# The last jobs of a DCN kernel reordered, its last phase taken into the run, and one group's output turned tile by tile

## The chip, the core and the metric

One Trainium2 chip, one core. The metric is the device time of one execution in microseconds (us), the median of several. An engine here is one of five: PE is TensorE (matmuls), ACT is ScalarE, DVE is VectorE, POOL is GpSimd, SP is SyncE, which in this kernel issues nearly all transfers (DMAs).

## The reference

A deep and cross network: six layers, each multiplies the running x by a weight matrix, adds a bias, multiplies by the first input and adds x.

```python
B, F, D, L = 16384, 26, 16, 6        # x0: 16384 x 416, all bfloat16
x = x0
for l in range(6):
    proj = jnp.einsum('bd,de->be', x, ws[l]) + bs[l]
    x = x0 * proj + x
return x
```

## The kernel before

**Layout.** The 16384 rows are cut into 8 groups of 2048, and x is kept transposed: features on partitions, rows along the free axis. 416 features are three tiles of 128 and a tail of 32. A *job* (g, l) is layer l of group g. It has 3 *tiles* of output features, each of 4 *chunks* of 512 columns (512 rows of the batch). The four 32-feature tails of a group's four chunks share one 128-partition tile `x3s`, one quadrant each. In some layers the quadrants stand rotated, and a copy of the tail is then rotated by two DMAs (`rotate`, lines 444 and 445), issued in `prefill`.

**Evacuation.** A chunk's sum of 13 row matmuls (or 3 full ones and a small one) lands in a PSUM bank. ScalarE adds the bias and writes it to `tw` (lines 514 and 550); VectorE multiplies it by x0 (L523, L562) and adds x (L528, L567). That is the chunk of x for the next layer. Tails go the same way through `ts` (L604 to L612).

**The run.** Most tiles are computed in one long *run* (`stream`). There a chunk isn't four matmuls over the whole array but 13 matmuls of 32 rows by 128 columns (L1040, and L1044 for the tail features), and four such matmuls for different chunks are in work at once, one on each 32-row strip. Which chunk each strip takes next is written out by hand in the string `ORDER`: one letter is one strip's share of one chunk (its letter tells the strip and how many chunks back the chunk was begun), and `|` is a *phase*, at which the tails of a batch of jobs (three, at the end two) are computed in one go (`tails`, L697 and L685). `replay` walks through the string and works out in units of 1/20 of a matmul's time when each letter starts, when each PSUM bank comes free, and so the order in which matmuls are emitted. Its constants (READ, NEXT, SUMS and so on) are the planner's estimates of what an evacuation takes.

The run ends with (7,4) tile 0, the item called `behind`; the last four chunks of the run get their three full-width matmuls behind it (`full`, L650). After the run come five more tiles in whole-array matmuls: (6,5) tiles 0 and 1, a phase with the tails of (7,4) and (6,5), (6,5) tile 2, and (7,4) tiles 1 and 2.

**The last job.** (7,5) is computed the other way round (L1130), with the rows of the batch on partitions, so that its result needs no turning. It multiplies and adds in that layout (`nat_mul`, L1188; `nat_add`, L1194) and stores (`nat_store`, L1201). For its residual it needs x(7,5) turned: tiles 0 and 1 by DMA transposes (`rest_turn`, L928), tile 2 by TensorE (`turn_last`, L1141).

**The outputs.** When the last layer of a group g < 7 is done, `output(g)` turns its three tiles by DMA transposes into `ost` (L880) and the tails into `ot3` (L888); `spread` copies `ot3` into its columns of `ost` on POOL (L909), for group 6 on ACT (L907); `store` writes `ost` to memory (L916). There is one `ost` for all groups. `done_with(g, l)` is called once for a job's tails and once for its tiles, and the second call starts `output`.

**What sets the order.** `Program` keeps one queue for each engine, in the order of the `add` calls, and turns reads and writes of named tokens into semaphore waits. Each engine works its queue in order, so an instruction that waits holds up everything behind it on that engine. For SyncE that means: a DMA whose data isn't ready holds up all later DMAs. In the last part its order is: turns of tiles 0 and 1 of group 6, `ot3`, two half turns of tile 2, two half turns of x(7,5) tile 1, then the two halves of store 6. On ScalarE the spread of group 6 stands between the evacuations of (7,4) tiles 1 and 2.

Of the kernel before, what the change touches and what calls it, by code (L numbers as in the profile page):

```python
# [21 lines left out]
class Program:  # L22
# [176 lines left out]

SLOT = 20  # L200
FENCE, PHASE, CHANGE = 22, 52, 9
READ, NEXT, BACK, SECOND, PAIR, TAILS, SUMS = 19, 56, 70, 92, 56, 220, 240
LETTERS = "ABCDEFGHIJKLMNOPQRSTUVWXYZabcdefghijklmnopqrstuvwxyz0123456789"
ORDER = (
    "ABCDAJCXaFTMWDUNSLYBKTMZjGANDaMpCPUJCXIROEDBaTUJCITVCQLVCAXNaALVaQHNKUTBQKDRICbRK|AJDWQJDCfUNSDM"
    "dSbJECbURCTINWDUJSPAJCTAZSPUJCDVYOTJAaDYVKTENCbNUSDJAXSYJGPAVODNUDOJUTCIRCDUNSbAJTaMVKHQBCXQNCPI"
    "ZSDJQCDMVaTEJOXBUDOAZXOIRGDYBSXARLOYBXKMZG|QBPSIVDCPAZOXQJGDQBaTINCLAdSXJYOHRACTNUCPJUSDAVCXRMaL"
    "FUCXARWPYBKPAdaLUNCLMVTCNISDcBWPIRCLAVSbMBKPYVSHMB|CTMVCPIVCDUNaTIBaTVAKTNUGDMVSDINCXYJCDMVSbIFW"
    "PQBCTMVCPIVSDIBWTANKTYVODAZOTUJGDURODINCbUJODBMSbIVCTUBSPIVGDQVCTMJWDAZSXINGDUBSXIBKTAZKPcRGAZPW"
    "QBP|QBOLRECTBCUPZSAPRaXASJPUBKUDVSAPRKAbSNcDOUbFKDURKDIRCbQJOXBIODVAOTUJCLQVCDUNSbEJWDQVCTINCbUJ"  # L210
    "ODIBaTVAKTNUGDMVSDINCXBcXSNAKPAZWLAVKTYNGDYNSDYN|ICXJTACVQPCNAPeVAPeRYLWNQDKNbCIBWTYBSLMVCLMVCXM"
    "JSDAdWPQBLOQBbKNQCDdMWTZEODNUKTABOXAVCTcVOLERCDcRaPAJWbMRKHYBCXQNCPIZSDJQCDMVaDMJSbAJTOYVGDMVCjU"
    "N|ISDJTAKRMDJCQDNeITVGMbBWIDRWIDRKAbJSMDBObQJCDdOQXJaMDJWMTBKAXhSMDJOUDVKQPFCMDBaQfVKALRWMDJOUDV"
    "KATBOYjREWDROULBKUTBSIBLCUdCMLZSAbJSUDRKMXeFLQBCXMR|CPISFDQCTIBaDUZKDQJWbMBXOIZCLQBSbIdODIVCTUJO"
    "DIVODIBbCNYXKERDCUdTaIBTaJUOHAVCTMVKDUJSDAVCXQNKDYJWfAJWTMZGDMVCXcNS|IDJTECRCTANaDYVKTMFWDUBOXAN"
    "KXZQODZATOJUCLURODINCbIBWTJYOHAVCTMVKDUJSDIRDCUNSbBISbVAKPURCLMRWDINCXIBWTJgOHAVCTMVKDUJSDAVCXQN"
    "KDYJSfAJaPURGDMdCbUN|ISDJTECRCTANaDMVKTFYWDAVOTYJGXAVODNUDOJUTCIRODIBSbUJPCIVDQCZTMBaLMBaXIBWLQZ"
    "ODIZCXQZKPAJWDRMWDNUKTBISBDUORbAOZDaULNQGXJCQXBAWPRaIDRKUDJSUPGBAbVCMDVOYLFSUPBeMXRCM|RCPISFDQCT"
    "IBaTIVOHQBPCMVDOAZWPBUOLQBCfURODIdWPQZGDQNCbINWDINXGQBPAWBQPKVDIVSPAJODYJCXQKZPEBWDQNWLAVKTAJSAD"
    "OVYDNKTYBKbMVSHBeMXRCM|RCPISFDQCDMVaTIBSbUBTKMVCLMVSDIBSXIZDKURDSMJCbIBSXIZOHQBCTMVCPIVSDQJCTIBa"  # L220
    "DUZSLAJbQOVHAOBbUOBLUChTIVOALVOQDJCXQBiLMSVDKMBbWJMHCVASXdIDJSUPCJUDSVIDSBMbRCMLRCcbJOALVMaDJMaD"
    "JYOXRAO|ANXKQBLSABOXYRGLMVDWNACbNQWDNISDJAWfBcSXJMGbVQCPRCPISFDAeTUBKTMVCLUNSDMJTCIBWTIdOHQBPCMV"
    "DOAZWPBUKDQVCfIRWPYFCXQZCPIRWDJQWPEBCTAZSPUJCLAZCXMRaLUBWLAVLSgNXGIRCDUNS|IDJTAKRMDJCQbJWATVCQPJ"
    "WALBaUTBODUadTIGVATVOIDJWAXRKYPFCMDBaMTCZMLRWALRCAfROUDJeUTaBQPKVEDVSMDJOAfJCQXKZMDJWATJWMDVKMTB"
    "CARaXMBKPZUDWRIPaAJbCYVTO|EJDWQBPCNAbOVLQCJDUiRLaAJbSUNDKMXCBMTWJYHOAVPCMVDOUBPWIRDIORXENKLAUKBN"
    "CD"
)


def replay(tails, events, needs, keep, part):  # L230

# [10 lines left out]
    n = len(tails)  # L242
    size = [[(3 if c < n - keep else part) + (r == tails[c]) for r in range(4)] for c in range(n)]
    free, flight, begun, act = [0] * 4, {}, 0, 156
    banks = [(0, 0), (0, 1), (0, 2), (0, 3), (84, 4), (84, 5), (178, 6), (178, 7)]
    home, read, out, latest, due = {}, {}, [], [[]] * 4, list(events)

    def over(now):
        nonlocal act
# [8 lines left out]
    for letter in ORDER:  # L258
        if letter == "|":
            now, m = min(free), due.pop(0)  # L260
            parts = [(f - now) // SLOT for f in free]
            at = now + max((f - now) % SLOT for f in free)
            over(at)
            on = at + 3 * SLOT * m + PHASE
            moved = [on + SLOT * k for k in parts]
            for f in flight.values():
                f[1] = moved[f[2]] if f[1] == free[f[2]] else -9 * SLOT
            got = [banks.pop(0) for _ in range(m)]
            assert all(t <= at + 3 * SLOT * k for k, (t, _) in enumerate(got))
# [12 lines left out]
            out.append([at, -1, [b for _, b in got], on])  # L282
            continue
        age, r = divmod(LETTERS.index(letter), 4)
        c, now = begun - age, free[r]
        over(now)
        if not age:
            t, home[c] = banks.pop(0)
            start, begun = max(now, t), begun + 1
            for t, d in needs[c]:  # L290
                start = max([start] + [read[d + k] + SUMS - SLOT * t for k in range(4)])
            flight[c] = [sum(1 << q for q in range(4) if size[c][q]), 0, r]
        else:
# [12 lines left out]
def bass_standalone__cross_network_dcn__recsys_kernel(  # L306
# [18 lines left out]
             (0, 4), (1, 3), (2, 2), (3, 1), (0, 5), (1, 4), (2, 3), (3, 2), (4, 0), (1, 5),  # L325
             (2, 4), (3, 3), (4, 1), (5, 0)]
    order += [(NG - 1 - g, L - 1 - l) for g, l in reversed(order)]
    order[-6:] = [(5, 5), (7, 3), (6, 4), (7, 4), (6, 5), (7, 5)]
    assert len(set(order)) == NG * L
    cuts = [1, 2, 3] + [3] * 12 + [3, 2]  # L330
    batches = []
# [206 lines left out]
    def evacuate_chunk(g, l, i, j, b, read):  # L538
# [138 lines left out]
    def tails(batch, corners_last=False, banks=None):  # L677
# [26 lines left out]
        if corners_last:  # L704
            corners()
            for k in sorted(range(len(batch)), key=lambda k: k != 1):
                evacuate_tail(*batch[k], bs_[k], vector=k == 1)
                while behind_tail:
                    behind_tail.pop(0)()
        pr.flush()  # L710
        for g, l in batch:
            if corners_last:
                prefill(g, l + 1)
                filled.add((g, l + 1))
            done_with(g, l)
        while later:
            load_group(later.pop(0))
# [155 lines left out]
            add("sp", lambda h, j=j: h.dma_start(brow[j * T32:j * T32 + 1, :], bs[L - 1:L, :]),  # L873
                reads=["brow"], writes=[("brow", j)], lane="brow", batch=0)

    def output(g):

        s, s3 = xset[(g, L)], xtail[(g, L)]
        def turn(t, j0=0, j1=NJ):
            add("sp", lambda h: h.dma_start_transpose(  # L880
                ost[:, j0 * KK:j1 * KK, t * P:(t + 1) * P], xs[s][:, t * GC + j0 * CH:t * GC + j1 * CH]),
                reads=[("x", s, t, j) for j in range(j0, j1)], writes=[("ost", t, j) for j in range(j0, j1)],
                lane="ot" if g < LAST - 1 else f"ot_{t}{j0}", batch=g)
# [4 lines left out]
        add("sp", lambda h: h.dma_start_transpose(ot3[:, :, :], x3s[s3][:, :]),  # L888
            reads=[("x3", s3)], writes=["ot3"], lane="ot3", batch=g)
# [53 lines left out]
        if (jb, i) in where:  # L943
            items.append(("tails", where[(jb, i)]))

    for i in range(1, NT):
        late = items.index(("tile", (LAST, L - 2), i))
        items.append(items.pop(late))


    single = 0
    k = 0
    while k < len(items):
        if items[k][0] == "tails":
            if single % 2 == 0:
                nxt = k + 1
# [48 lines left out]
    def stream(run, keep, part):  # L1005
# [72 lines left out]
    for n, it in enumerate(items):  # L1078
# [200 lines left out]
```

## Time and profile before

| | |
|---|---|
| median of 3 runs | 467.53 us (467.3 to 467.93) |
| profiled execution | 467.5 us, of which 465.7 are the span from first to last instruction |
| run (L1040, L1044), first to last start | 40.74 to 429.14 us |
| start of (7,5) on TensorE | 448.50 us |
| TensorE, VectorE, ScalarE busy | 458.9, 404.2, 379.1 us |
| transfers | 53.77 MB; 256-byte packets from the turns, 832-byte packets from the stores |

Times are counted from the span's start. A line of the timeline reads: start, length, engine, source line, operation, what it writes and reads, count of merged instructions, and in brackets the idle time before it and what ended it. For SPq lines the length is that of the issue on SyncE, not of the transfer; when a transfer lands is read from the semaphore that it raises. PE's ends are modelled, so starts are used for its pace.

### The profile page before, as it was taken

To read this page: it belongs to the slowest core of one execution; us is meant where nothing else is said; L and a number is where in the kernel's file an instruction comes from. 1 tells how busy PE (TensorE), PEld (TensorE's weight loads), DVE (VectorE), ACT (ScalarE), POOL (GpSimd) and SP (SyncE) were. 2 spreads that over 40 slices of the span, in tenths; PEclk is the share of its full clock that TensorE was granted. 3 is DMA by queue.
4 is the path that set the end of the run, shared out by engine and by line. 5 is a ranking of instruction groups with operands and counts; after the bars stand their busy time and mean duration, and the time that the engine had idled before them with its cause. 6 is when DMAs were issued, how large, how long until landed. Compare 5 with 4: busy or idle time off the path is not lost.

```text
span 465.7 us, 17469 instructions
## 1 busy us (share of the span) xinstructions
PE 458.9 (99%) x7827; PEld 263.8 (57%) x7833; DVE 404.2 (87%) x700; ACT 379.1 (81%) x608; POOL 6.8 (1%) x15
## 2 busy tenths in 40 slices
PE   9999999999999999999999999999999999999995
PEld 5444566555556677555655556565575566755442
DVE  2887998989989899979989898888989889898897
ACT  4687888788888888888878888788887887889785
POOL 1000000000000000000000000000000000000000
PEclk9999999999999999999999999999999999999998
DMA  8986949101002978084858437990100095027899
GB/s 229 185 177 144 160 113 190 29 3 26 1 4 38 158 210 155 22 141 149 149 92 154 145 78 141 160 296 23 25 2 4 25 148 172 14 49 169 183 161 292
DMA packets 139087, 53.77 MB, mean 115 GB/s; under 512 B 112762, under 2 KB 138500, under 8 KB 139012
## 3 DMA queue, kind: packets, MB, share of 16 engines
q1 hardware_dynamic: 138856, 52.54, 52.5%
q8 instruction: 61, 1.00, 0.9%
q10 hardware_dynamic: 156, 0.11, 0.1%
q14 instruction: 14, 0.11, 0.1%
HBM read 5.97 MB, written 13.63 MB: 42 GB/s over the span
## 4 chain that ended last, share of the span: by engine, by line
PE 93%; DVE 4%; DMA 1%; issue 1%; ACT 0%; SPq 0%; DVEq 0%
PE ps L1040 70%; PE ps L697 7%; PE ps L1044 6%; PE ps L650 6%; PE ps L638 2%; PE ps L685 1%; DMA wm<-in_ws_dram 1%; DVE x L1194 1%; DVE x L1188 1%; DVE x L528 1%; DVE tw L523 1%; PE ps L671 1%; ACT tw L514 0%; PE ps L789 0%; SPq L734 0%
## 5 line engine op out<-in xcount | busy, mean ns | idle before, releaser
L1040 PE MATMUL ps<-x,wm 32*128 32x512 bf16 x6000 | 356.0, 374 | 0.0
L550 ACT ACTIVATE tw<-ps,bias 128x512 bf16<-128x512 f32 x500 | 310.5, 688 | 46.4 <-PE ps L1040 35.9
L1040 PEld LDWEIGHTS ps<-x,wm 32*128 32x128 bf16 x6000 | 212.5, 92 | 127.7 <-ACT tw L550 4.1
L562 DVE TENSOR_TENSOR tw<-tw,x 128x1024 bf16<-128x1024 bf16 x250 | 168.2, 689 | 39.6 <-ACT tw L550 38.9
L567 DVE TENSOR_TENSOR x<-tw,x 128x1024 bf16<-128x1024 bf16 x250 | 163.5, 690 | 0.3
L1044 PE MATMUL ps<-x,w 32*128 32x512 bf16 x504 | 151.7, 374 | 0.0
L1044 PEld LDWEIGHTS ps<-x,w 32*128 32x128 bf16 x504 | 42.7, 92 | 6.6
L514 ACT ACTIVATE tw<-ps,bias 128x512 bf16<-128x512 f32 (+1 forms) x46 | 35.0, 839 | 12.0 <-PE ps L671 7.9
L650 PE MATMUL ps<-x,wm 128*128 128x512 bf16 x146 | 33.6, 379 | 1.0 <-issue 0.8
L697 PE MATMUL ps<-x,wm 128*32 128x512 bf16 x564 | 33.6, 380 | 0.0
L608 ACT ACTIVATE ts<-ps,bias 128x512 bf16<-128x512 f32 x33 | 21.0, 687 | 14.7 <-PE ps L685 14.7
L523 DVE TENSOR_TENSOR tw<-tw,x 128x1024 bf16<-128x1024 bf16 (+1 forms) x35 | 21.4, 627 | 4.9 <-ACT tw L514 4.7
L650 PEld LDWEIGHTS ps<-x,wm 128*128 128x128 bf16 x152 | 13.9, 98 | 19.0 <-issue 3.2
L697 PEld LDWEIGHTS ps<-x,wm 128*32 128x32 bf16 x564 | 13.5, 96 | 18.7 <-ACT tw L550 4.7
L528 DVE TENSOR_TENSOR x<-tw,x 128x1024 bf16<-128x1024 bf16 (+1 forms) x35 | 20.6, 624 | 0.0
L612 DVE TENSOR_TENSOR x<-ts,x 128x512 bf16<-128x512 bf16 x47 | 18.4, 420 | 0.4
L610 DVE TENSOR_TENSOR ts<-ts,x 128x512 bf16<-128x512 bf16 x33 | 13.0, 418 | 0.0
L604 DVE SCALAR_TENSOR_TENSOR ts<-ps,bias,x 128x512 bf16<-128x512 f32 x14 | 10.5, 748 | 2.2 <-PE ps L685 2.2
L909 POOL COPY ost<-ot 128x512 bf16<-128x512 bf16 x6 | 5.3, 890 | 411.3 <-DMA ot<-x 411.3
L1130 PE MATMUL ps<-wm,x 128*128 128x416 bf16 x48 | 9.8, 340 | 0.1
L1182 ACT ACTIVATE x<-ps 128x416 bf16<-128x416 f32 x16 | 7.6, 518 | 2.4 <-PE ps L1130 2.4
L799 DVE COPY x<-ps 128x512 bf16<-128x512 bf16 x5 | 2.0, 423 | 8.5 <-PE ps L789 8.5
(50 smaller groups left out, 76.9 us busy)
## 6 DMA issues: line engine op xcount, KB each, us to landing
out_dram<-ost SPq DMA_DIRECT2D x6, 1664.0 KB, 7.1
x<-x SPq DMA_DIRECT2D x24, 96.0 KB, 2.3
x<-in_x_dram SPq DMA_DIRECT2D x8, 208.0 KB, 4.4
x<-in_x_dram SPq DMA_DIRECT2D x4, 416.0 KB, 8.0
out_dram<-ost SPq DMA_DIRECT2D x2, 832.0 KB, 6.0
wm<-in_ws_dram SPq DMA_DIRECT2D x5, 312.0 KB, 3.4
x<-x SPq DMA_DIRECT2D x22, 64.0 KB, 2.0
out_dram<-x SPq DMA_DIRECT2D x3, 416.0 KB, 4.8
```

The source lines that it names most:

```text
L514: add("act", lambda h, a=a, w=w, b0=b0: h.activation(tw[r][:, a * CH:(a + w) * CH], psum[:, b0 * CH:(b0 + w) * CH], ACT_F.Identity, bias=b ...
L523: add("dve", lambda h, a=a, e=e: h.tensor_tensor(tw[r][:, a * CH:e * CH], tw[r][:, a * CH:e * CH], x0s[s0][:, i * GC + a * CH:i * GC + e * ...
L528: add("dve", lambda h, a=a, e=e: h.tensor_tensor(xs[so][:, i * GC + a * CH:i * GC + e * CH], tw[r][:, a * CH:e * CH], src(i, a, e), ALU.ad ...
L550: add("act", lambda h: h.activation(tw[r][:, j * CH:(j + 1) * CH], bank(b), ACT_F.Identity, bias=bias[:, i, l:l + 1], scale=1.0), reads=[( ...
L562: add("dve", lambda h: h.tensor_tensor(tw[r][:, o], tw[r][:, o], x0s[s0][:, c], ALU.mult), reads=[("tw", r, k) for k in both] + [x0_tok(s0 ...
L567: add("dve", lambda h: h.tensor_tensor(xs[so][:, c], tw[r][:, o], src(i, a, a + 2), ALU.add), reads=[("tw", r, k) for k in both] + [stok(i ...
L608: add("act", lambda h: h.activation(ts[r][:, :], bank(b), ACT_F.Identity, bias=bias[:, 3, l:l + 1], scale=1.0), reads=[("ps", b), "bias"], ...
L612: add("dve", lambda h: h.tensor_tensor(x3s[so][:, :], ts[r][:, :], res, ALU.add), reads=[("ts", r)] + rtok, writes=[("x3", so), ("x3", so, ...
L650: add("pe", lambda h, t=t, j=j, k=k, w=w: h.matmul(bank(banks[j])[:, k * w:(k + 1) * w], wm[l][:, t, ecols], src(t, j, j + 1)[:, k * w:(k ...
L697: add("pe", lambda h, t=t, j=j, src=src, l=l, b=b, ro=ro, qo=qo: h.matmul(psum[qo, b * CH:(b + 1) * CH], wm[l][:, t, NT * P:D], src(t, j, ...
L1040: add("pe", lambda h, l=l, t=t, j=j, b=b, q=q, ecols=ecols, src=src, kw=kw: h.matmul(bank(b), wm[l][q, t, ecols], src(t, j, j + 1)[q, :], ...
L1044: add("pe", lambda h, l=l, b=b, q=q, ecols=ecols, s3=s3, kw=kw: h.matmul(bank(b), w3[l][q, ecols], s3[q, :], **kw), reads=tok3 + [("w3", l ...
```

## The change

The order of the last eight jobs becomes (6,3) (5,5) (7,2) (6,4) (7,3) (6,5) (7,4) (7,5), where (6,5) stood behind the first tile of (7,4) before. The tails' last batches are written out to match, and the string `ORDER` is made anew behind its first 89 letters. It has 516 chunks instead of 504 and 15 phases instead of 14: the three tiles of (6,5) and the phase of two tails are now in the run, and behind the run only (7,4) tiles 1 and 2 are left. `replay` gets a list `after`: a chunk whose job needs tails of an earlier phase is not begun until ROTATE = 600 units behind that phase.

In `tails`, all rotations of a batch (`prefill`) are issued ahead of the outputs that the batch completes. The turns of groups 5 and 6 are issued tile by tile as each tile is finished (`finish_tile`), the last tile of group 6 in two halves; `output` of these groups issues `ot3` only, which for group 6 stands behind all its turns. The spread and the store of group 6 move to the point behind (7,4) tile 0, ahead of the turns of x(7,5).

```diff
--- before.py
+++ after.py
@@ -199,35 +199,36 @@
 
 SLOT = 20
 FENCE, PHASE, CHANGE = 22, 52, 9
-READ, NEXT, BACK, SECOND, PAIR, TAILS, SUMS = 19, 56, 70, 92, 56, 220, 240
+READ, NEXT, BACK, SECOND, PAIR, TAILS, SUMS, ROTATE = 19, 56, 70, 92, 56, 220, 240, 600
 LETTERS = "ABCDEFGHIJKLMNOPQRSTUVWXYZabcdefghijklmnopqrstuvwxyz0123456789"
 ORDER = (
-    "ABCDAJCXaFTMWDUNSLYBKTMZjGANDaMpCPUJCXIROEDBaTUJCITVCQLVCAXNaALVaQHNKUTBQKDRICbRK|AJDWQJDCfUNSDM"
...
+    "ABCDAJCXaFTMWDUNSLYBKTMZjGANDaMpCPUJCXIROEDBaTUJCITVCQLVCAXNaALVaQHNKUTBQKDRICbRK|AJDWQJDKbQBSDQ"
...
 )
 
 
-def replay(tails, events, needs, keep, part):
+def replay(tails, events, needs, after, keep, part):
+
 
 
 
@@ -243,7 +244,7 @@
     size = [[(3 if c < n - keep else part) + (r == tails[c]) for r in range(4)] for c in range(n)]
     free, flight, begun, act = [0] * 4, {}, 0, 156
     banks = [(0, 0), (0, 1), (0, 2), (0, 3), (84, 4), (84, 5), (178, 6), (178, 7)]
-    home, read, out, latest, due = {}, {}, [], [[]] * 4, list(events)
+    home, read, out, latest, due, past = {}, {}, [], [[]] * 4, list(events), []
 
     def over(now):
         nonlocal act
@@ -262,6 +263,7 @@
             at = now + max((f - now) % SLOT for f in free)
             over(at)
             on = at + 3 * SLOT * m + PHASE
+            past.append(on)
             moved = [on + SLOT * k for k in parts]
             for f in flight.values():
                 f[1] = moved[f[2]] if f[1] == free[f[2]] else -9 * SLOT
@@ -287,6 +289,8 @@
         if not age:
             t, home[c] = banks.pop(0)
             start, begun = max(now, t), begun + 1
+            if after[c] is not None:
+                start = max(start, past[after[c]] + ROTATE)
             for t, d in needs[c]:
                 start = max([start] + [read[d + k] + SUMS - SLOT * t for k in range(4)])
             flight[c] = [sum(1 << q for q in range(4) if size[c][q]), 0, r]
@@ -325,7 +329,7 @@
              (0, 4), (1, 3), (2, 2), (3, 1), (0, 5), (1, 4), (2, 3), (3, 2), (4, 0), (1, 5),
              (2, 4), (3, 3), (4, 1), (5, 0)]
     order += [(NG - 1 - g, L - 1 - l) for g, l in reversed(order)]
-    order[-6:] = [(5, 5), (7, 3), (6, 4), (7, 4), (6, 5), (7, 5)]
+    order[-8:] = [(6, 3), (5, 5), (7, 2), (6, 4), (7, 3), (6, 5), (7, 4), (7, 5)]
     assert len(set(order)) == NG * L
     cuts = [1, 2, 3] + [3] * 12 + [3, 2]
     batches = []
@@ -334,6 +338,7 @@
         batches.append(order[n:n + c])
         n += c
     assert n == NG * L - 1
+    batches[-3:] = [[(5, 4), (6, 3), (7, 2)], [(5, 5), (6, 4), (7, 3)], [(6, 5), (7, 4)]]
 
 
     XW = NT * GC
@@ -572,7 +577,7 @@
 
         todo = [multiply, plus]
         if len(out_) == NJ:
-            todo.append(lambda: finish_tile(g, l))
+            todo.append(lambda: finish_tile(g, l, i=i))
         while todo:
             if behind_tail or phases and max(dve[0], ready[(g, l, i, a)]) + PAIR > phases[0] + 14:
                 behind_tail.extend(todo)
@@ -708,10 +713,10 @@
                 while behind_tail:
                     behind_tail.pop(0)()
         pr.flush()
+        for g, l in batch if corners_last else ():
+            prefill(g, l + 1)
+            filled.add((g, l + 1))
         for g, l in batch:
-            if corners_last:
-                prefill(g, l + 1)
-                filled.add((g, l + 1))
             done_with(g, l)
         while later:
             load_group(later.pop(0))
@@ -873,28 +878,29 @@
             add("sp", lambda h, j=j: h.dma_start(brow[j * T32:j * T32 + 1, :], bs[L - 1:L, :]),
                 reads=["brow"], writes=[("brow", j)], lane="brow", batch=0)
 
-    def output(g):
-
-        s, s3 = xset[(g, L)], xtail[(g, L)]
-        def turn(t, j0=0, j1=NJ):
-            add("sp", lambda h: h.dma_start_transpose(
+    def turn(g, t):
+
+        s = xset[(g, L)]
+        halves = ((0, 2), (2, NJ)) if (g, t) == (LAST - 1, NT - 1) else ((0, NJ),)
+        for j0, j1 in halves:
+            add("sp", lambda h, j0=j0, j1=j1: h.dma_start_transpose(
                 ost[:, j0 * KK:j1 * KK, t * P:(t + 1) * P], xs[s][:, t * GC + j0 * CH:t * GC + j1 * CH]),
                 reads=[("x", s, t, j) for j in range(j0, j1)], writes=[("ost", t, j) for j in range(j0, j1)],
                 lane="ot" if g < LAST - 1 else f"ot_{t}{j0}", batch=g)
 
-        turn(0)
-        if g == LAST - 1:
-            turn(1)
+    def output(g):
+
+        s, s3 = xset[(g, L)], xtail[(g, L)]
+        if g < LAST - 2:
+            turn(g, 0)
         add("sp", lambda h: h.dma_start_transpose(ot3[:, :, :], x3s[s3][:, :]),
             reads=[("x3", s3)], writes=["ot3"], lane="ot3", batch=g)
         if g < LAST - 1:
             spread("pool")
-            turn(1)
-            turn(2)
+            if g < LAST - 2:
+                turn(g, 1)
+                turn(g, 2)
             store(g, 0, NJ)
-        else:
-            turn(2, 0, 2)
-            turn(2, 2, NJ)
         free_x.append(s)
         free_3.append(s3)
 
@@ -931,8 +937,8 @@
                 writes=[("x5n", j, t) for j in range(j0, j1)], lane=f"x5_{t}{j0}", batch=0)
 
     items = []
-    where = {(b[0 if b in batches[4:-3] else min(1, len(b) - 1)], 0): b for b in batches[:-1]}
-    where[((LAST - 1, L - 1), 1)] = batches[-1]
+    where = {(b[0 if b in batches[4:-3] else min(1, len(b) - 1)], 0): b for b in batches[:-3]}
+    where.update({((5, 4), 1): batches[-3], ((6, 4), 1): batches[-2], ((6, 5), 1): batches[-1]})
     behind = ("tile", (LAST, L - 2), 0)
     del where[((0, 0), 0)]
     where[((0, 1), 0)] = where.pop(((1, 0), 0))
@@ -943,14 +949,9 @@
         if (jb, i) in where:
             items.append(("tails", where[(jb, i)]))
 
-    for i in range(1, NT):
-        late = items.index(("tile", (LAST, L - 2), i))
-        items.append(items.pop(late))
-
-
     single = 0
     k = 0
-    while k < len(items):
+    while items[k] != ("tile", (0, 2), 1):
         if items[k][0] == "tails":
             if single % 2 == 0:
                 nxt = k + 1
@@ -960,7 +961,7 @@
                     k += 1
             single = 0
         else:
-            single = 1 if items[k] == behind else single + 1
+            single += 1
         k += 1
 
     W_LOAD = {(1, 0): 3, (0, 2): 4, (1, 1): 5}
@@ -979,7 +980,9 @@
 
     tiles_done = {}
 
-    def finish_tile(g, l, n=1):
+    def finish_tile(g, l, n=1, i=None):
+        if l == L - 1 and g > LAST - 3:
+            turn(g, i)
         tiles_done[(g, l)] = tiles_done.get((g, l), 0) + n
         if tiles_done[(g, l)] == NT:
             done_with(g, l)
@@ -1015,8 +1018,9 @@
         place = {it: NJ * k for k, it in enumerate(tiles)}
         needs = [[(t, place[(g, l - 1), t]) for t in range(NT if c < len(chunks) - keep else part)
                   if c - place.get(((g, l - 1), t), -99) < 30] for c, ((g, l), i, j) in enumerate(chunks)]
+        phase = {jb: k for k, (n, b) in enumerate(due) for jb in b}
         plan, read, left = replay([quad(g, l, j)[0] for (g, l), i, j in chunks], [len(b) for n, b in due],
-                                  needs, keep, part)
+                                  needs, [phase.get((g, l - 1)) for (g, l), i, j in chunks], keep, part)
         at = list(ring)
         plan = [(t, r, c, at[b]) if r >= 0 else (t, r, [at[k] for k in c], b) for t, r, c, b in plan]
         left = [at[k] for k in left]
@@ -1108,8 +1112,10 @@
                 evacuate(g, l, i, banks, list(range(NJ)), 2)
         finish_tile(g, l)
         if (g, l) == (LAST, L - 2) and i < NT - 1:
-            if i:
+            if not i:
                 spread("act")
+                store(LAST - 1, 0, 2)
+                store(LAST - 1, 2, NJ)
             rest_turn(i)
 
 
@@ -1206,8 +1212,6 @@
     a0, a1, a2, a3 = bka = take(NJ)
     b0, b1, b2, b3 = take(NJ)
     bks = {0: bka, 1: [b0, b1, b2, a0], 2: [a1, a2, a3, b3], 3: [b0, b1, b2, a0]}
-    store(LAST - 1, 0, 2)
-    store(LAST - 1, 2, NJ)
     for j in range(NJ):
         nat_full(0, j, bks[0][j], True, (0, 1))
     turn_tails(b0)
```

More of the change, by code (lines that the diff above doesn't have):

```diff
@@ L201 @@
 FENCE, PHASE, CHANGE = 22, 52, 9
-READ, NEXT, BACK, SECOND, PAIR, TAILS, SUMS = 19, 56, 70, 92, 56, 220, 240
+READ, NEXT, BACK, SECOND, PAIR, TAILS, SUMS, ROTATE = 19, 56, 70, 92, 56, 220, 240, 600
 LETTERS = "ABCDEFGHIJKLMNOPQRSTUVWXYZabcdefghijklmnopqrstuvwxyz0123456789"
 ORDER = (
-    "ABCDAJCXaFTMWDUNSLYBKTMZjGANDaMpCPUJCXIROEDBaTUJCITVCQLVCAXNaALVaQHNKUTBQKDRICbRK|AJDWQJDCfUNSDM"
[L206 to L226, printed above, removed]
@@ new lines @@
+    "ABCDAJCXaFTMWDUNSLYBKTMZjGANDaMpCPUJCXIROEDBaTUJCITVCQLVCAXNaALVaQHNKUTBQKDRICbRK|AJDWQJDKbQBSDQ"
+    "dKbMFCbMVSDMJCXIZSDJAXSIBKTYBSLUZDKMVTCMJSDIZOTEBPCUBPSAZLCRUKDdQaXJAWTYJGPAVODNUDOJUTCIBCbUNKDI"
+    "daTMVCPJUaTFA|RODMLFCAXYSBPQCZPIWRALROUDKBQXaJATKVASLVMCLBYSXNICDZMWDVMSDNICfVISbBSbJUOHAVCTMVKD"
+    "UJSDIRPCANbCVMSLYBLORUHBeMXRCM|RCPISFDAWTIBKDUZKDgRKbMVCXJMaTFAODVATOJUCLURODARCfYRWLARXOANLYBaL"
+    "QVCLcNSXEKRDAWNDUOJTAKRATCNDUaNLcGBTMWZHSBMbCVM|RCPISFDQCDMVaTIBSbUBTKMVCLMVSDANSXAdTOJUDJCYTVAO"
@@ new lines @@
+    "BPcWJDUeRbIGVPCUBTMWBPIWRDICTVCMJDWcRLaMXFCMTBaIDVSIPFCUPRCADRaUPFKQDaNQXCIBXSIZHOQBPCMVLCAZDaRM"
+    "DaNIXCVcTOJYXSFA|RODMLFCAXYSBPQCZPIWRALROUDKBQXaJATKVASLVMGDBYSXJATCZMSLVEODNUCDRAafJQPGBbMCZULS"
+    "BIeTZODIVCTUJODIVODIBbCNYXCIVSPAdaLUBWLMRHKBYXRCM|RCPISFDQCDMVaTEJOXBUPCAZPSUBPKQVDKQBTaAZKDQZKX"
+    "MFSDYBXOAdKXQNCLMZSDINTCANWDVgSLENXKBUTCAVPYCVLMSBDMeVLSYFXCMVTCMJDWIZPSFAPCUBPSIVHCURPCMBaDMZLC"
+    "IVTaMFDOYVDMJWfAVK|MBXKNALWNQCDNQCbJAWTBQePJCfQZWPERCPAWJPgSHARCTYNKDUJSDIRPCANbSBYSLVATKUNCLMVS"
@@ new lines @@
+    "DINCXIBWTJgOHAVCTMVKDUJSDAVTCMRbKUBWLARWLYNTGIVCDUNS|IDJTAKRMDJCQbJWALVSMDNKAbJCUTBeIPSVDKURPCJM"
+    "DaVIDSBMbRKUHBSMXBOIDZCMTZCYTNWAPJWQDRKATJaUPCJUDSVIDSJUDRKAbJSAbRKUHOBUDOBYXORIDKQZDSMJXCAZDWQN"
+    "bGUBPWANLSUZDKMVbCUN|ISDJTECRCTANaDMVKTFYWDAVOTYJGXAVODNUDOJUTCIRODIBSbUBTKMVCLMVSDANCbUdDSINXaF"
+    "QDCRcXKZMTFAaDRWMLBKUTBSIBLCUZCMXZSAPJSUDRKMXeFLQBCXMR|CPISFDQCDMVaTIFCbAVOTYJWHAVCTUNKDUJSDIRPC"
+    "IBbCYVKDQVaLMFWDVAOXRIbGBQODYNCPIVCXQJODANTCMZeTANSLYFPUCVMLSBLASBPQCdPISVHAORDYNKDANeTUFKMbCVLA"
@@ new lines @@
+    "RWDMJSDYRKDANWbICVbAORLYWBLWMRHBOcXRCM|RCPISFDAWTIBKDUZKDgRKbMVCXJMaTFAODVATOJUCLURODARCfYRWLARX"
+    "OANLYBaLQVCLcNSXEKRDAWNDUOJTAKRATCNDUaNLcGBTMWZHSBMbCVM|RCPISFDQCDMVaTIBSbUBTKMVCLMVSDANSXAdTOJU"
+    "DJCYTVAOBPcWJDUeRbIGVPCUBTMWBPIWRDICTVCMJDWcRLaMXFCMTBaIDVSIPFCUDVSAPBWMbKBULCRcLWEZTOAZDSNUDOJU"
+    "TCIRDSIBbSUJDCMZXKQBTCMdLWAVLeMRHCNYXSEB|ODUNLAKVDANWbQFKUPCVMDBaMVDWINTCANfSIDdaQXJGYPBWIPCVIDB"
+    "aMDZWMLRCIbBWQbBSIPZWALVOQDJOAXKBUTdCQLNWEDVODANaTCYNfSVEDSNUDNKUTBKMTBaIDRCMTZCYTNWAPJWQDRKMDJa"
@@ L227 @@
+    "UPCJAbSVIDSJUDRKUPBKAbRWMDJCYTVOIHBAaXBQOLVcGDVQODJMeXRAK|MBXKNALWNQCDNAWbJAWTBSPcJUGbNQKHVEOLBC"
+    "DANCXMKBLYCVTYeNHAaVfQGJ|ADCRUbCJTAgSJbMiVLQWBTMVCD"
 )
-def replay(tails, events, needs, keep, part):
+def replay(tails, events, needs, after, keep, part):
     n = len(tails)
```

## The prediction

> **What bounds the kernel now.** I read the page first: its engines and its chain.
>
> ```profile
> PE 458.9 (99%) x7827; PEld 263.8 (57%) x7833; DVE 404.2 (87%) x700; ACT 379.1 (81%) x608; POOL 6.8 (1%) x15
> ...
> PE 93%; DVE 4%; DMA 1%; issue 1%; ACT 0%; SPq 0%; DVEq 0%
> ```
>
> TensorE sets the time. Between two phases, from 388.23 to 413.40 us, the trace has 468 matmuls of lines 1040 and 1044, one each 53.9 ns; a quarter of a full tile's 216 ns (L650). So the run has no holes that a new order could close, and only the end can move by much. The timeline of TensorE shows the end:
>
> ```profile
> 428.93 0.59 PE L1040 MATMUL ps<-x,wm 32*128 32x512 bf16 x2
> ...
> 439.64 2.76 PE L638 MATMUL ps<-x,wm 128*32 128x512 bf16 x48
> ...
> 448.50 1.80 PE L1130 MATMUL ps<-wm,x 128*128 128x416 bf16 x8
> ...
> 458.45 2.28 PE L1130 MATMUL ps<-wm,x 128*128 128x416 bf16 x12
> ```
>
> The run's last matmul starts at 429.14, the last job (7,5) at 448.50, and PE ends at 460.7. VectorE's timeline shows that it has no slack there either:
>
> ```profile
> 454.39 1.08 DVE L1194 TENSOR_TENSOR x<-x,x 128x832 bf16<-128x832 bf16 x2
> ...
> 461.75 0.65 DVE L1194 TENSOR_TENSOR x<-x,x 128x416 bf16<-128x416 bf16 x2
> ```
>
> From the second add of nat_add (454.90) it works without a gap until 462.40, 7.5 us, and the last store lands 2.75 us after its issue at 462.15. Now ScalarE, which evacuates, and SyncE, which issues all transfers in one order:
>
> ```profile
> 442.76 4.75 ACT L514 ACTIVATE tw<-ps,bias 128x1024 bf16<-128x1024 f32 x7 [0.98 <-PE ps L671]
> 447.54 0.63 ACT L907 ACTIVATE ost<-ot 128x512 bf16<-128x512 bf16 x1
> 448.07 2.41 ACT L514 ACTIVATE tw<-ps,bias 128x512 bf16<-128x512 f32 x4
> ```
>
> ```profile
> 427.55 0.41 SPq L916 DMA_DIRECT2D out_dram<-ost  x1
> 428.00 1.96 SPq L444 DMA_DIRECT2D x<-x  x1
> ...
> 444.57 1.69 SPq L888 DMA_TRANSPOSE ot<-x  x1
> 446.39 2.62 SPq L880 DMA_TRANSPOSE ost<-x  x2
> 449.05 2.72 SPq L928 DMA_TRANSPOSE x<-x  x2
> 451.95 1.87 SPq L916 DMA_DIRECT2D out_dram<-ost  x2
> ```
>
> The spread (L907) needs ot3, issued at 444.57 and landed at 447.52: ScalarE came to it at 447.51 and waited for nothing. The two turns of x(7,5) tile 1 (L928) land at 453.75 and 454.62, and the adds that read them start at 454.39 and 454.90: they are in time by 0.6 and 0.3 us. Both waits are met with almost nothing to spare, and the change moves both. Last, the packets in two windows, 449 to 454 and 454 to 464:
>
> ```profile
> DMA packets 3093, 0.79 MB, mean 158 GB/s; under 512 B 3092, under 2 KB 3092, under 8 KB 3092
> ...
> DMA packets 4211, 3.37 MB, mean 337 GB/s; under 512 B 175, under 2 KB 4211, under 8 KB 4211
> ```
>
> Store 6 is issued at 451.95, but its 832-byte packets start only when the 256-byte packets of the turns ahead are through. The queue works in order. The 96 KB rotation issued at 428.00 behind store 5 says the same: it landed at 434.71, after the store (434.37), where its line's median is 2.0 us.
>
> **The change, part by part** (times on the clock of before).
>
> *Three tiles and a phase of two go into the run.* Before, tiles (6,5) and their tails take TensorE from 432.14 to 442.57: 10.4 us. In the run they are 12 chunks of 13 matmuls, 156 x 53.9 ns = 8.4 us, and a phase. A phase of three takes 2.71 us from last to next run matmul (413.40 to 416.11); a third tail's 12 matmuls of L697 at 49.9 ns are 0.6 us, so a phase of two costs 2.1. Sum 10.5 us: even, +0.1. The run's last matmul comes at 429.14 + 10.5 = 439.6. Tiles 0 to 2 of (7,4) follow as now, 3.0 us each, and (7,5) could start at 448.6.
>
> *New order, and ROTATE.* From a phase to the first chunk that needs its tails, the letters hold at least 120 matmuls before and 119 after: 6.4 us, while the last tail add ends 2.7 us after its phase (416.11 to 418.84). Cost nothing; cover 3.7 us. I bound the pace of the run by its own stretches, 53.7 to 54.4 ns: +-0.7 us, and take 0.
>
> *Rotations ahead of the outputs of a batch; group 5 turned tile by tile.* Four rotations (0.6 us of issue each) now come before ot3 of group 5 and its store, which moves from 427.55 to about 430 and lands at 436.9. The first turn of group 6, which writes the same buffer, waits for its data until about then. Nobody waits: 0.
>
> *ot3 of group 6 behind all its turns; the spread a tile earlier.* Before, the last full tile of the run has its final add done 3.65 us after the run's last matmul (432.79 against 429.14). (6,5) tile 2 now has that place: 443.3. SyncE then issues two half turns (1.23 and 1.34 us) and only then ot3, at about 445.9; it lands 3.0 later, 448.9. ScalarE comes to the spread when (7,4) tile 0 is evacuated, 3.94 us after the run (433.08 before): 443.6. It stands still for 5.3 us. Behind it are the eight evacuations of tiles 1 and 2, and behind those PSUM banks for (7,5), VectorE and TensorE. The spread keeps ScalarE 0.53 us, so tile 1's first evacuation starts at 449.4 instead of 445.09: **+4.3 us**. The first matmuls of (7,5) read tile 1's sums, so TensorE shifts likewise, to an end at 465.0. Bounds: data 2.4 to 3.9 us after the run give 3.1 to 4.7.
>
> *Store 6 ahead of the turns of x(7,5).* Its two halves need the spread (449.5) and the last half turn (issued 444.6, landing 3.4 later). They go out at 449.6. Store 5, of the same 1664 KB, put its first packet 1.0 us after issue and the last after 5.9 us. Behind it stand 4096 packets of tiles 0 and 1 of x(7,5); turns move 213 GB/s (434 to 440), or 832 packets per us, so 4.9 us; landing follows the last packet by 0.5. Second half of tile 1: 449.6 + 5.9 + 4.9 + 0.5 = 460.9. The add that reads it was at 454.90: **+6.0 us**. This is not added to the 4.3: the add waits for the later of the two. Behind it on VectorE stand all the remaining multiplications and adds, the 7.5 us without a gap, and nothing catches up. Even with no stall at the spread, the half turn's landing holds the stores to 448.0, so +4.4 would remain.
>
> [...]
>
> *End.* The last 104 KB stores now meet an empty queue: 2.3 us as a 96 KB x<-x, not 2.75: -0.3 taken, bounds 0 and -0.5.
>
> **Sum:** +6.0 - 0.3 = +5.7, and 0.1 for the run: +5.8. The profiled execution took 467.5 us, a span of 465.7 and 1.8 around it; the median of the runs is 467.53, the same. Forecast 467.5 + 5.8 = **473.3 us**.
>
> **Rivals.**
>
> *The store doesn't hold the turns back.* If x(7,5) passes it, only the spread's 4.3 stays: 471.8, and 470.6 at its lower bound of 3.1. The two rows on packets and the rotation speak against it. Chance 0.09. [...]
>
> *The TensorE clock drops.* TensorE waits about 4 us from 448.6 with one matmul in between. In this trace the granted clock is 1.00 until 463 and 0.5 after 463.2, 2.5 us behind the last matmul; at the start matmuls of 512 columns come every 418 ns from 0.8 to 3.3 us and every 216 from 6.1, so half speed lasts up to 5 us. That is 2.5 us of work lost: a shift of 4.3 + 2.5 = 6.8 on TensorE's path, past the 6.0: 474.3, at worst 475. Chance 0.12. [...]
>
> *Faster: the store out of the last stores' way.* Before, the DMA engines are full from 454 to 464 with store 6 and the final stores together, whose first takes 5.75 us to land. If store 6 were through early, the last landing gains 0.5 us, and (6,5) in the run spares the 2.6 us of gaps that VectorE had between 435 and 445, worth 0.1 to 0.4 where TensorE is full: 466.6 to 466.9. It decides where x(7,5) still lands by 454.9, that is with the store issued by 454.9 - 11.3 = 443.6. But tile 2 of (6,5) has its sums only at 443.3, with 2.6 us of issue and 3.4 of landing to come. Chance 0.05.
>
> *The order costs more than counted*, with holes at its new phase: 1 to 3 us on top, 474 to 476. The even pace of before speaks against it: 0.04. *All of it hidden*, 467.5: 0.02.
>
> **How the numbers follow.** The forecast gets the other 0.68. Its own range is 472.3 to 474.5. The whole range reaches from the spread alone at its lower bound, 470.6, to a store as slow as L916's slowest (8.9 instead of 6.8, +2.1), 475.4, and a little of a dip or a hole: 475.8. A change of 0.2% (0.9 us) is about what a measurement of this kernel can tell from none. Slower: 0.68 + 0.09 + 0.12 + 0.04 = 0.93; same 0.02; faster 0.05.
>
> **What would show it.** ScalarE idle for about 5 us ahead of the spread, released by DMA ot<-x; ot3 issued behind the two half turns; store 6 issued at about 449.6 and L928 right behind it, the last landing near 461 and over 6 us after issue; VectorE idle ahead of L1194 with a DMA as releaser; the run's pace at 53.7 to 54.4 ns. I am wrong if ot3 lands before ScalarE needs it, or if L928 lands within 5 us of issue behind the store.

## The result, and the profile after

The changed kernel takes 475.06 us (median of four, 474.62 to 475.64) against 467.69 for the kernel before beside it: a ratio of 1.0159, 95% interval 1.0141 to 1.0177. That is 7.4 us slower. The span of the profiled execution grew from 465.7 to 473.0, by 7.3 us, and its own time is 475.64.

Engines and chain, from the page of the changed kernel:

```profile
PE 462.6 (98%) x7893; PEld 268.3 (57%) x7893; DVE 404.1 (85%) x700; ACT 379.4 (80%) x609; POOL 6.2 (1%) x15
...
PE 93%; DVE 4%; issue 1%; DMA 1%; ACT 1%; SPq 0%; DVEq 0%
```

Shares of the span hide it: 7 us are 1.5% of everything. The timeline of ScalarE at the end shows where they start:

```profile
441.78 2.44 ACT L519 ACTIVATE tw<-ps,bias 128x512 bf16<-128x512 f32 x4
450.18 0.63 ACT L913 ACTIVATE ost<-ot 128x512 bf16<-128x512 bf16 x1 [5.96 <-DMA ot<-x]
450.71 4.72 ACT L519 ACTIVATE tw<-ps,bias 128x512 bf16<-128x512 f32 x8
```

ScalarE was through with tile 0 of (7,4) at 444.22 and then stood still for 5.96 us until ot3 had landed (450.16). The eight evacuations behind the spread started at 450.71, where tile 1's first was at 445.09 before. TensorE's timeline shows what waited for them:

```profile
445.68 2.76 PE L655 MATMUL ps<-x,wm 128*128 128x512 bf16 x12
451.44 0.35 PE L1136 MATMUL ps<-wm,x 128*128 128x416 bf16 x1 [2.99 <-ACT tw L519]
454.50 2.61 PE L1136 MATMUL ps<-wm,x 128*128 128x416 bf16 x7 [2.71 <-DVE x L533]
...
466.79 2.28 PE L1136 MATMUL ps<-wm,x 128*128 128x416 bf16 x12
```

One matmul of (7,5) at 451.44, when a bank came free; the rest from 454.50, when the sums of tile 1 were there. The last group starts at 466.79, where it was 458.45 before: 8.3 us later, although TensorE's own start is only some 6 us later (454.50 against 448.50). The rest is in the clock. Two windows show it; behind the window and its length stand the busy times (and counts) of PE, its weight loads, DVE, ACT and POOL, then the granted clock, the share of the DMA engines and GB/s:

```profile
448.50:453.50 5.00, 0.35 (x1) 0.10 (x1) 1.04 (x2) 3.32 (x6) 0.00 (x0) 1.00 0.53 150
453.50:460.35 6.85, 5.85 (x31) 2.95 (x32) 4.53 (x12) 2.59 (x6) 0.00 (x0) 0.50 1.01 259
```

From 453.52 to 460.35 TensorE had half its clock, nearly all of it with work to do: the seven matmuls from 454.50 come every 343 ns instead of 177.

SyncE, and the adds of VectorE that read the turned x(7,5):

```profile
447.52 1.28 SPq L896 DMA_TRANSPOSE ot<-x  x1
450.83 1.00 SPq L922 DMA_DIRECT2D out_dram<-ost  x2
451.93 9.21 SPq L934 DMA_TRANSPOSE x<-x  x3
463.83 7.01 SPq L1207 DMA_DIRECT2D out_dram<-x  x5
```

```profile
460.05 0.69 DVE L1156 COPY x<-ps 128x1024 bf16<-128x1024 bf16 x1 [2.32 <-PE ps L1147]
461.07 0.69 DVE L1156 COPY x<-ps 128x1024 bf16<-128x1024 bf16 x1 [0.33 <-PE ps L1147]
461.68 1.12 DVE L1194 TENSOR_TENSOR x<-x,x 128x832 bf16<-128x832 bf16 x2
462.71 1.09 DVE L1200 TENSOR_TENSOR x<-x,x 128x832 bf16<-128x832 bf16 x2
...
470.09 0.65 DVE L1200 TENSOR_TENSOR x<-x,x 128x416 bf16<-128x416 bf16 x2
```

Store 6 goes out at 450.83, the turns of x(7,5) stand behind it, and their last half lands at 462.94. The add that reads it starts at 463.22 (454.90 before) and has no idle time ahead of it: VectorE came to it straight from work that TensorE had held back (the copies at 460.05 and 461.07, released by PE). So two things end within 0.3 us of each other, and the profile names only one. The experiments take them apart.

### The profile page after: what moved, and what is told of

Its sections match the earlier page's. It is cut to its first block, busy times and chain, and to the rows that moved or that the text cites. A ratio compares the mean times of both kernels' runs of the same rounds, so it can differ in the third digit from the quotient of the medians.

```text
span 473.0 us, 17586 instructions
## 1 busy us (share of the span) xinstructions
PE 462.6 (98%) x7893; PEld 268.3 (57%) x7893; DVE 404.1 (85%) x700; ACT 379.4 (80%) x609; POOL 6.2 (1%) x15
## 4 chain that ended last, share of the span: by engine, by line
PE 93%; DVE 4%; issue 1%; DMA 1%; ACT 1%; SPq 0%; DVEq 0%
PE ps L1044 70%; PE ps L702 7%; PE ps L1048 6%; PE ps L655 4%; PE ps L643 1%; PE ps L690 1%; DVE x L1200 1%; PE ps L1136 1%; DVE x L1194 1%; PE ps L776 1%; PE ps L794 1%; DVE x L572 1%; DVE tw L567 1%; DMA ot<-x 1%; PE ps L676 1%
## 5 line engine op out<-in xcount | busy, mean ns | idle before, releaser
L1044 PE MATMUL ps<-x,wm 32*128 32x512 bf16 x6144 | 364.4, 374 | 0.0
L555 ACT ACTIVATE tw<-ps,bias 128x512 bf16<-128x512 f32 x512 | 318.7, 688 | 49.6 <-PE ps L1044 36.5
L1044 PEld LDWEIGHTS ps<-x,wm 32*128 32x128 bf16 x6144 | 219.4, 92 | 129.0 <-PE ps L1044 4.0
L567 DVE TENSOR_TENSOR tw<-tw,x 128x1024 bf16<-128x1024 bf16 x256 | 172.0, 688 | 42.4 <-ACT tw L555 41.2
L572 DVE TENSOR_TENSOR x<-tw,x 128x1024 bf16<-128x1024 bf16 x256 | 167.1, 690 | 0.2
L519 ACT ACTIVATE tw<-ps,bias 128x512 bf16<-128x512 f32 (+1 forms) x36 | 27.9, 860 | 8.1 <-PE ps L676 7.0
L655 PE MATMUL ps<-x,wm 128*128 128x512 bf16 x128 | 29.9, 382 | 0.0
L528 DVE TENSOR_TENSOR tw<-tw,x 128x1024 bf16<-128x1024 bf16 (+1 forms) x29 | 17.3, 613 | 8.3 <-ACT tw L519 8.1
L533 DVE TENSOR_TENSOR x<-tw,x 128x1024 bf16<-128x1024 bf16 (+1 forms) x29 | 16.7, 610 | 0.0
L1136 PEld LDWEIGHTS ps<-wm,x 128*128 128x128 bf16 x48 | 4.6, 106 | 11.3 <-ACT tw L519 3.5
```

The lines of the kernel that those rows point to most:

```text
L519: add("act", lambda h, a=a, w=w, b0=b0: h.activation(tw[r][:, a * CH:(a + w) * CH], psum[:, b0 * CH:(b0 + w) * CH], ACT_F.Identity, bias=b ...
L528: add("dve", lambda h, a=a, e=e: h.tensor_tensor(tw[r][:, a * CH:e * CH], tw[r][:, a * CH:e * CH], x0s[s0][:, i * GC + a * CH:i * GC + e * ...
L555: add("act", lambda h: h.activation(tw[r][:, j * CH:(j + 1) * CH], bank(b), ACT_F.Identity, bias=bias[:, i, l:l + 1], scale=1.0), reads=[( ...
L567: add("dve", lambda h: h.tensor_tensor(tw[r][:, o], tw[r][:, o], x0s[s0][:, c], ALU.mult), reads=[("tw", r, k) for k in both] + [x0_tok(s0 ...
L572: add("dve", lambda h: h.tensor_tensor(xs[so][:, c], tw[r][:, o], src(i, a, a + 2), ALU.add), reads=[("tw", r, k) for k in both] + [stok(i ...
L655: add("pe", lambda h, t=t, j=j, k=k, w=w: h.matmul(bank(banks[j])[:, k * w:(k + 1) * w], wm[l][:, t, ecols], src(t, j, j + 1)[:, k * w:(k ...
```

## The experiments

**e1: store 6 behind the turns again.**

```diff
             if not i:
                 spread("act")
-                store(LAST - 1, 0, 2)
-                store(LAST - 1, 2, NJ)
             rest_turn(i)
...
+    store(LAST - 1, 0, 2)      # ahead of the last job's first matmuls, as before
+    store(LAST - 1, 2, NJ)
```

> The changed kernel with one part undone: the two halves of store 6 are issued behind the turns of x(7,5) again, as before; the spread on ScalarE stays at its new place. Theory A (two gates): the end is set by the later of two gates, TensorE's (the 5.96 us stall of ScalarE at the spread, 5.6 us on the first evacuation of tile 1, and then half clock from 453.52 to 460.35, 2.7 us) and the turns of x(7,5) behind the store (second half landed at 462.94, 0.28 us before its add at 463.22). TensorE's gate is the later one, so undoing the store alone changes nothing: 475.0 us, at least 474.6. Rival B (the forecast on record: the store ahead of the turns sets the end): 470.5 to 471.5. Rival C (the spread and the clock alone, the store is harmless): 475.0 as well; it is told from A by e2.

474.20 us, ratio 1.0146 (1.0131 to 1.0161). The interval overlaps that of the changed kernel, though the time is 0.4 us below the 474.6 that theory A had set as the least. The last half turn now lands at 459.25, four microseconds ahead of its add, and of the 7.4 us 6.8 stay: the store's place isn't what ends last there. Rival B falls. TensorE has the same gap and the same half clock:

```profile
453.50:460.30 6.80, 5.56 (x30) 2.83 (x31) 4.48 (x12) 2.83 (x6) 0.00 (x0) 0.50 0.68 164
```

**e2: the spread on POOL.**

```diff
-                spread("act")
+                spread("pool")
```

> The changed kernel with the spread of group 6 on POOL, which is idle there, instead of ScalarE; the store stays ahead of the turns of x(7,5). ScalarE has nothing to wait for any more, so TensorE starts (7,5) at about 448.3 and its clock stays at 1.00. Theory A (two gates): the turns still land at about 462.9, so VectorE stands idle some 8 us less its work ahead of nat_add, and the end moves by 0.3 us at most: 474.5 to 475.1. Rival B: the same. Rival C (spread and clock alone): 467 to 468.

475.74 us, ratio 1.0183 (1.0158 to 1.0209). Again nothing is won; two of its four runs, at 476.5 and 477.1, lie above anything expected, and why is open. TensorE starts (7,5) at 448.71, keeps its clock at 1.00 and is through at 461.1, as before the change. VectorE's timeline says why that is worth nothing:

```profile
453.87 1.10 DVE L1194 TENSOR_TENSOR x<-x,x 128x832 bf16<-128x832 bf16 x2
462.31 0.59 DVE L1200 TENSOR_TENSOR x<-x,x 128x832 bf16<-128x832 bf16 x1 [7.35 <-DMA x<-x]
463.45 0.59 DVE L1200 TENSOR_TENSOR x<-x,x 128x832 bf16<-128x832 bf16 x1 [0.55 <-DMA x<-x]
```

It waits 7.35 us for the turns behind the store. Rival C falls with this, and each of the two parts alone leaves the loss nearly whole.

**e3: both undone.**

```diff
-            if not i:
-                spread("act")
-                store(LAST - 1, 0, 2)
-                store(LAST - 1, 2, NJ)
             rest_turn(i)
+            if not i:
+                spread("pool")
...
+    store(LAST - 1, 0, 2)
+    store(LAST - 1, 2, NJ)
```

> The changed kernel with both undone: spread of group 6 on POOL, behind the memset for the turns, and store 6 behind the turns of x(7,5). Theory A: both gates open; the turns (4096 packets behind the turns of group 6, whose packets end at 449.4) land at 455.4 to 456, 0.5 to 1.3 us later than the adds need them, so 467.5 to 469. Rivals B and C: each would have come back with its own part alone, and this gives the same 467.5 to 469 as that part.

468.65 us, ratio 1.0027 (1.0016 to 1.0038): 1.2 us over the kernel before beside it, so 6.2 of the 7.4 us are gone. Theory A holds.

**e5: e1 with TensorE kept at work.**

```diff
+            if (g, l, i, t, j) == (LAST, L - 2, NT - 1, NT - 1, NJ - 1):
+                for _ in range(24):   # zero is a [128, 128] tile of zeros
+                    add("pe", lambda h: h.matmul(bank(banks[j]), zero[:, :], one, start=False, stop=False), ...)
```

> e1 (store behind the turns, spread on ScalarE) with 24 matmuls by a tile of zeros ahead of the last matmul of the last tile of (7,4): they add nothing to the sum and keep TensorE at work in the 6.2 us in which it waited. If the half clock costs what its rows say (6.8 us of half speed, of which 5.8 with work, 2.9 us of work lost), the time falls by 2.5 to 2.9 us against e1, to 472.1 to 472.6. If the half clock hid behind other waits: 475.0 as e1.

472.82 us, ratio 1.0114 (1.0099 to 1.0129), 1.4 us under e1 by the medians and 2.3 by the spans of the profiles (473.1, which was e1's longest, to 470.8). The gap is filled and the clock stays:

```profile
447.87 5.39 PE L651 MATMUL ps<-const-bfloat16-1.0,zero 128*128 128x512 bf16 x23
453.10 0.38 PE L659 MATMUL ps<-x,wm 128*128 128x512 bf16 x1
...
453.50:460.00 6.50, 6.06 (x58) 3.34 (x58) 6.50 (x15) 4.55 (x11) 0.00 (x0) 1.00 0.77 189
```

TensorE's last matmul starts 3.3 us earlier than in e1 (465.58 against 468.85; 0.65 of that is an earlier start at 454.09). Of this 0.9 us is given back at the end: the last stores now follow store 6 closely, and the last on SyncE lands 2.65 us after its issue instead of 1.72. So the half clock does cost, less than the expected 2.5 to 2.9 in the time. The earlier start isn't the edit's: in e1's profile store 5 (that of group 5) landed 2.0 us later (439.42 against 437.42), and the turns of group 6 and `ot3` came late with it. Without these 0.65 us the profiles differ by 1.7, near the 1.4 of the medians.

**e9: the kernel before, with the store ahead of the turns alone.**

```diff
             if i:
                 spread("act")
+                store(LAST - 1, 0, 2)
+                store(LAST - 1, 2, NJ)
             rest_turn(i)
...
-    store(LAST - 1, 0, 2)
-    store(LAST - 1, 2, NJ)
```

> The kernel before with one part of the change alone: the two halves of store 6 issued ahead of the two half turns of x(7,5) tile 1 (tile 0 was turned long before). Job order, spread and ot3 stay as before, so TensorE starts (7,5) at 448.5 and keeps its clock. The stores go out when the last half turn of group 6 has landed, 451.0; their packets pass from 452 to 457, those of the two half turns from 457 to 459.5; the second lands at 460 and its add moves from 454.9 to 460. With a last store that meets an empty queue (1.0 us less): 471.5, range 470.8 to 472.3. If the store ahead of the turns were harmless by itself: 467.4.

471.24 us, ratio 1.0077 (1.0062 to 1.0092), as expected: half of the change's loss from one swap in SyncE's order, in the old job order and with TensorE untouched. VectorE:

```profile
454.11 1.14 DVE L1190 TENSOR_TENSOR x<-x,x 128x832 bf16<-128x832 bf16 x2
459.98 0.59 DVE L1196 TENSOR_TENSOR x<-x,x 128x832 bf16<-128x832 bf16 x1 [4.74 <-DMA x<-x]
```

**e6 and e7: ot3 issued early.** Both are e3 with ot3 of group 6 issued at the phase that makes its tails; e6 has the spread on POOL, e7 on ScalarE at the place that the change gave it.

```diff
         for g, l in batch:
+            if (g, l) == (LAST - 1, L - 1):
+                turn_3(g)             # the issue of ot3, taken out of output(6)
             done_with(g, l)
```

> e3 (spread on POOL, store 6 behind the turns of x(7,5)) with ot3 of group 6 issued at the phase that makes its tails, behind the turn of tile 0, where SyncE stood idle for 0.8 us, instead of behind the last half turn. If e3's last 1.2 us over the kernel before come from the transfers queued ahead of the turns of x(7,5) (its adds waited 0.67 and 0.76 us for them), the turns land 1.3 us earlier, the waits go, and the time is 467.0 to 467.6, level with before: the job order then costs nothing by itself. If the 1.2 us come from the new order of the run or from the last stores meeting store 6, 468.3 to 468.7.

> e6 with the spread on ScalarE at the place that the changed kernel gives it, behind tile 0 of (7,4). The place is harmful only because ot3 lands late: issued early it lands at about 445 to 446, ScalarE comes to it at 444.2 and waits 1 to 2 us instead of 5.96, TensorE waits about as long and its clock has no reason to drop. 467.5 to 469; if a spread at this place costs ScalarE's stall whatever ot3 does, 473 or more.

e6: 468.34 us, ratio 1.0021 (1.0012 to 1.0029), at the lower edge of the second of its two expectations and clear of the first. But the first wasn't put to the test: the last half turn landed only 0.7 us earlier than in e3 (455.40 against 456.08), not 1.3. e7: 468.68, ratio 1.0022 (1.0013 to 1.0032). In e7 ScalarE waits 0.47 us at the spread, less than the 1 to 2 expected: the place is harmless, it was ot3's place behind two half turns that made it cost 5.96. What is left over the kernel before is 0.9 us, which e6 didn't settle: VectorE still waited for the turns,

```profile
455.49 0.59 DVE L1204 TENSOR_TENSOR x<-x,x 128x832 bf16<-128x832 bf16 x1 [0.82 <-DMA x<-x]
```

and its last store landed 2.9 us after issue.

**e8, e10, e11: what the last microsecond is.** e8 puts the turns of x(7,5) ahead of group 6's last two half turns; e10 and e11 leave store 6 out of e6 and of the kernel before.

```diff
             rest_turn(i)              # e8
             if not i:
                 spread("pool")
+            else:
+                turn(LAST - 1, NT - 1)   # and not in finish_tile
```

> e6 with the two half turns of tile 2 of group 6 issued behind the turns of x(7,5) instead of ahead of them (store 6 stays last). In e6 VectorE still waited 0.13 and 0.82 us for the turns of x(7,5), and its 0.9 us over the kernel before could be that. Theory D (the transfers as a whole set the end: in e6 the 16 DMA engines are full from 444 to 465, and the last store lands 2.9 us after its issue instead of 1.7): VectorE's waits go, the last store waits that much longer in the queue, 468.0 to 468.6. Theory E (VectorE's waits set the end): 467.2 to 467.6.

> e6 without store 6: the rows of group 6 are turned but not stored. Theory D: the last stores meet an empty queue and land 1.0 to 1.2 us sooner; VectorE's waits for the turns of x(7,5) stay, so 467.1 to 467.4. Theory E (the waits alone): 468.2 as e6.

> The kernel before without store 6 (the rows of group 6 are not stored): what a store that is out of the way of the last stores could bring at most. VectorE's chain is unchanged to 462.4 and the last store lands 1.7 us after its issue, as in the changed kernel, not 2.75: 466.4 to 466.6. If the last stores don't feel it: 467.4.

e8: 469.13 us, ratio 1.0038 (1.0025 to 1.0052). VectorE no longer waits for the turns (they land at 452.01 and 453.35), and the time doesn't fall: it comes out 0.8 us above e6, with intervals that overlap a little, and beyond the 468.6 that I gave. The last store on SyncE is issued at 461.98 and lands 4.8 us later. e10: 467.28, ratio 1.000 (0.999 to 1.001). e11: 466.40, ratio 0.9982 (0.9972 to 0.9991).

Theory E falls with e8 and e10. Theory D fits e8: VectorE waits for no DMA, and the last store takes its 4.8 us with the DMA engines at a share of 0.93 (289 GB/s) from 455 to 467. But e10 doesn't bear out D alone. Without store 6 its last store lands 1.74 us after issue, as e11's does (1.73), and yet e10 stands 0.9 us above e11. That difference is VectorE's (its last add ends at 463.67, against 462.60 in e11), which waits for the turns of x(7,5) with or without the store:

```profile
454.96 0.59 DVE L1204 TENSOR_TENSOR x<-x,x 128x832 bf16<-128x832 bf16 x1 [0.76 <-DMA x<-x]
456.22 0.59 DVE L1204 TENSOR_TENSOR x<-x,x 128x832 bf16<-128x832 bf16 x1 [0.67 <-DMA x<-x]
```

So store 6 costs the old order and the new one alike 1.0 us, and the 0.9 us of e6 over the kernel before aren't its. In e6 they are mostly such waits: VectorE's last add ends 0.5 us later than in the kernel before (462.94 against 462.40), while the last store takes 0.2 us more to land. In e8 VectorE is through at 461.98, and the last store pays instead. The likely reason, which no run tests alone, is that the new job order gives the DMA engines more to move late: x(7,5) tile 0 is turned at 448 to 452 in e6, where the old order turned it at 435.23 to 439.96, in a stretch in which the DMA engines had little else to do (their share is 0.57 from 435 to 440, against 1.03 from 439 to 455 in e6). And e11 bounds what a store out of the way could bring the old order: 1.0 us. No version here that stores every row beats the kernel before.

## Why the prediction was right, and where its steps were off

The direction, the two places and the time within the whole range were right; 7.4 us were measured where 5.8 were forecast. The forecast's own range, 472.3 to 474.5, was missed, and the wait that it let come last wasn't the one that came last. That the total still came out near is in part luck: as e2 shows, the path that was named leads to about the same end as the one that wasn't.

*The run.* Right. Its last matmul starts at 439.32 (forecast 439.6), the stretches between phases keep 53.8 to 54.5 ns except the short ones at the end (55.3 and 54.9 ns), and as far as the run goes (7,5) could have started at 448.3.

*The spread.* The mechanism was right and the size short: a stall of 5.96 us, not 5.3, and 5.6 on tile 1's first evacuation, not 4.3. ScalarE came to it later (444.22, not 443.6), and so did ot3 (issued at 447.52, not 445.9). The term that failed is the data of tile 2: I took it as the start of the half turn at 443.3. The sums were there at 444.0, and SyncE came free only at 444.75, since the turn of tile 1 ahead took 3.1 us to issue, not the 2.0 that is the median of its line. (The upper bound of 4.7 for this step adds up to 4.6; nothing hangs on it.)

*The store ahead of the turns.* Right as a mechanism, by e2 and e9, and 2.0 us short: the last half landed at 462.94, not 460.9. The later spread is 1.2 of this. Of the rest, some 0.4 is the store's last packet, 6.3 us after issue and not 5.9, and about half a microsecond is the issue: the whole turn of tile 0 behind the store took SyncE 6.5 us to issue (451.93 to 458.41), so the halves behind it were issued late, and the DMA engines ran dry near 459.5 (0 GB/s from 459.55 to 459.70).

*The slow store in the whole range.* It is L916's slowest in the kernel before, issued at 383.32 and landed 8.94 us later (store 5: 6.83). Store 6 landed 6.87 us after it was issued at 450.83: the slow store didn't come.

*Which of the two comes last.* Here the forecast chose wrongly. It let the turns set the end and gave the fall of the clock a chance of 0.12, at 474.3. The clock did fall, and with 5.6 + 2.7 us TensorE's path came out 0.3 us behind the turns' landing. The rule that the later one counts held: e1 and e2 each remove one and gain 0.6 us and nothing, e3 removes both and gains 6.2. The wait that I had worked out at 4 us with one matmul inside was 6.2.

*The signs.* Two of them didn't come out as written. VectorE was to stand idle ahead of L1194 (now L1200) with a DMA as releaser: it did so in e2, for 7.35 us, but not in the changed kernel, where TensorE came last. And the forecast was to be wrong if L928 (now L934) landed within 5 us of issue behind the store: the whole turn of tile 0 took 8.26 us, but the two halves landed 3.31 and 3.13 us after their issue. They were held back all the same, because SyncE issued them only at 458.45 and 459.81. The time from issue to landing didn't show it, because the issue itself was held: 6.5 us for the turn of tile 0.

*Nobody waits for store 5.* Not in the changed kernel's own profile, where it landed at 437.57 and the first turn of group 6 was issued at 438.43. But in the profiles of e1, e3, e6 and e10 it landed 8.2 to 8.4 us after issue instead of 7.0, at 438.56 to 439.42, and that turn was issued 0.06 us later. The term wasn't always nothing: that turn then came up to a microsecond late.

*The clock.* The half clock lasted 6.83 us (453.52 to 460.35), where the rival had taken up to 5 from the start of the program. When it fell, TensorE had stood for 3.0 us ahead of the lone matmul (451.44) and for 1.7 of the 2.7 us behind it; in the kernel before it fell 2.5 us after the last matmul.

*The order of the queue.* No run here shows the turns landing ahead of a store issued before them: the store's halves landed at 454.88 and 457.70, the turns from 460.19 on. But landings didn't always follow the order of issue. Among the small rotations of the kernel before, one issued at 431.43 landed (435.18) just ahead of one issued at 430.37 (435.32).

*The end.* The last store's landing fell from 2.75 to 1.72 us, a gain of 1.0 where 0.3 was taken. Sum: 8.3 - 1.0 = 7.3, the growth of the span.

*The faster rival.* Of its price, the 0.5 us at the last stores was half of the 1.0 that e11 shows. The 0.1 to 0.4 elsewhere agrees with e8, where VectorE is through at 461.98 instead of 462.40. Its condition, a store issued by 443.6, was missed by 7 us.

## What to carry to other kernels

Where an engine meets a transfer just in time, write down the margin before moving anything ahead of either: here two margins of 0.02 and 0.3 us carried the whole end of the kernel. Before putting a large store into a queue ahead of small transfers, look who waits for those: here, with a 1.7 MB store ahead of the turns, VectorE stood for 4.74 us in e9 and 7.35 us in e2. And where two waits end together, undoing one shows next to nothing: undo both before calling either harmless.

## What the hardware showed that I had not expected

The issue of a DMA transpose behind a 1.7 MB store held SyncE for 6.5 us (4.8 us for a half in e9) instead of 1.8 (1.3), and the two half turns behind it were issued only at 458.45 and 459.81. TensorE's clock fell to half even though one matmul ran in the middle of the gap (451.44), and it stayed there for 6.83 us of which 5.85 had work. How soon it fell differed: behind the last matmul it came after 2.5 us in the kernel before (460.73 to 463.20) and after 4.9 us in the changed kernel (469.07 to 474.00).
